# A new order of the first 170 steps of a fused attention and expert kernel

## The chip, the cores and the metric

One core of one Trainium2 chip runs the whole program. The metric is the time of one execution on the device in microseconds; the time before is the median of three runs.

## The reference

Eight sequences of 576 positions with 8 heads of 64 go through attention over a causal window of 64 positions. The result, 576 x 512 for each sequence, goes through one expert of eight: the mean over the positions picks the expert, and the whole sequence goes through it.

```
mask   = (rel >= 0) & (rel < 64)                     # rel = query position - key position
attn   = softmax(where(mask, q @ k.T / 8, -1e9))
x      = attn @ v                                    # heads side by side: (8, 576, 512)
e      = argmax(x.mean(axis=1) @ w_gate)             # one expert for each sequence
out[b] = prob[e] * (relu(x[b] @ w1[e]) @ w2[e])      # w1: 512 x 1024, w2: 1024 x 512
```

## The kernel before, in words

The program is a long list of short steps, `OPS`, written out as text. A loop at the end of the kernel takes the steps one by one, and each emits its instructions; every engine runs its own instructions in the order in which the list emits them. Waits are put in by the framework from the data, the buffers and the PSUM banks that the steps share. So the list is the schedule.

A batch `b` (a sequence) has five units: four pairs of heads for positions 0 to 511, and a tail unit for positions 512 to 575 of all heads. Units are counted through: unit 7 is pair 2 of batch 1, unit 9 the tail of batch 1. A step's name is a letter, sometimes the letter of an engine (`a` for ACT, `d` for DVE) or of a variant (`m`: the PSUM tile comes from the tag `mo` with three buffers and not from a tag with one; `b`: the mask is added by a matmul), and a number:

- Loads. `Qx` loads q (even x) or k (odd x) of batch x // 2, 512 KB in bf16, from GpSimd's queue; `Q0.48` loads heads 4 to 7 alone. `Y0.24` loads heads 2 and 3 of batch 0 in fp32 from SyncE's queue, and `Cd0.24` casts them. `Lx` loads a piece of v (five for a batch, the last of half the size), `tx` the tails of q and k (two transfers), `Wx` a quarter of the expert's weights (`W0` and `W1` of w1, `W2` and `W3` of w2 for batch 0). All but `Y` are issued by GpSimd.
- Set-up. `y`, `i`: the band of the mask and the identity, on GpSimd; `mb`, `Mb`, `z`: masks and zeroes on DVE.
- Attention of a unit. `T` transposes q and k on TensorE; `U` and `k` copy the transposed q and k out of PSUM; `S` makes the scores; `E` takes the exponentials (ACT); `K` multiplies by the mask (DVE), where `S` had no `b`; `l` sums the rows (TensorE); `n` and `R` make the reciprocal (ACT, a logarithm and an exponential); `A` multiplies by v (TensorE); `X` scales the result into `xm` (DVE). `Vb` copies v shifted by half a block, on DVE, and the main `A` steps of the batch need it.
- Gate of a batch. `g`, `j`, `G` pick the expert, `P` reads its number into a register of GpSimd, and the `W` steps of that batch can be issued only then.
- Experts. Each `c` is the next chunk of matmuls of the expert (line 461 and 470 for w1, 503 and 512 for w2), each `r` moves a finished chunk out of PSUM, each `O` stores a result.

What the prediction's steps touch are these rules of the buffers: the transposes without `m` share one PSUM buffer, the scores without `m` one pair of banks, the row sums one buffer (`lb`), the products without `m` one (`av`); `mo` has three, of which `S` with `m` takes two. Exponentials have four buffers, transposed q three.

```
        if 'm' in e:
            sp = [ps_m.tile([128, 512], FP32, tag="mo", name="s") for _ in range(2)]
...
        pe = apool.tile([128, 2, 8, 64], FP16, tag="pe", name="pe", bufs=4)
...
        nc.gpsimd.dma_start(
            out=tiles[b][:, lo:hi],
            in_=src[b, lo:hi, 0:SM].rearrange("h (p r) d -> p h (r d)", r=4))
```

Of the kernel before, what the change touches and what calls it, by code (L numbers as in the profile page):

```python
# [1 line left out]
OPS = (  # L2
    "Y0.24 Q0.48 Q1.48 Q0.2 Cd0.24 y i Q1.2 Y1.24 Q3 Cd1.24 z Tm3 Tm2 mb T0 Tm1 ka3 ka2 ka0 "
    "t0 Ud3 Ud2 Q2 Sb3 L0 L3 ka1 L1 L2 E3 Smb2 L4 Ud0 l3 Ud1 t1 S0 T4 E2 kd4 Ud4 n3 Smb1 E0 "
    "Mb K0 E1 R3 Q4 L9 Tm5 Sb4 Tm7 Tm8 Ud5 Q5 ka5 kd8 E4 L5 kd7 l1 n1 T6 l4 n4 Ud7 l2 Sb5 ka6 "
    "n2 R1 R4 l0 V0 A3 Ud6 L7 Am1 n0 E5 T9 X3 Am2 Ud9 S7 R2 L8 E7 Ud8 X1 R0 l5 X2 L6 n5 Smb6 "
    "A0 Am4 K7 ka9 E6 t2 X4 X0 Sb8 l7 g0 n7 T12 j0 Q6 Sm9 Tm10 G0 Ud12 kd12 E8 Ud10 H0 E9 "
    "Tm13 Tm11 R7 K9 l6 R5 ka10 Sb12 Ud11 ka13 V1 n6 Q7 l8 P0 Ud13 W0 I0 kd11 T14 Am5 A7 X7 "
    "A6 Ud14 kd14 L12 n8 X5 E12 R6 l12 n12 Sm14 X6 S11 l9 E14 Smb10 Tm17 E11 n9 T18 W1 Ud17 "
    "A9 W2 E10 S13 kd18 Ud18 L13 Tm15 Ud15 l10 Am8 R8 W3 kd15 ka17 T16 K14 L11 c X8 L14 n10 "  # L10
    "E13 R9 c ra X9 c R10 c rd c g1 K11 rd S17 j1 G1 ra ra c H1 L10 c rd l14 K13 c t3 ra c P1 "
    "n14 Q8 ra c c rd c V2 Ua16 c c ra ka16 l11 A10 X10 Am12 W4 c Q9 R12 X12 n11 ra W5 R11 "
    "A11 rd W6 T19 E17 c l13 n13 R13 Ua19 I1 X11 c Sm18 S15 K17 L15 rd E18 W7 R14 A13 c l17 "
    "ra X13 A14 c L16 L17 X14 g2 n17 Tm20 E15 ra kd19 c Ud20 ra L18 kd20 T22 S19 Sm16 E19 L19 "
    "j2 G2 c P2 t4 K15 E16 Q10 K18 c ra c W8 H2 ra ka22 c ra c c S20 l18 ra rd rd K16 c n18 "
    "Q11 K19 L21 ra Tm21 c c Ua21 Ud22 l16 W9 T23 R17 kd21 L23 V3 c c R18 c ra Am17 Ud23 n16 "
    "ra l15 E20 X17 L22 c R16 ka23 c rd n15 A18 c S23 X18 Sm21 K20 T24 kd24 ra R15 E21 L20 "
    "A16 c l19 L29 ra L24 W10 n19 Ud24 Am15 X16 A19 W11 R19 c X15 l20 E23 n20 L25 I2 c X19 rd "
    "L26 ra Tm26 c g3 K23 kd26 l23 Ud26 R20 c ra Sm22 n23 S24 j3 rd G3 E24 E22 T28 H3 K21 c "
    "Tm27 Ud28 P3 t5 ka27 kd28 l21 L28 rd n21 I3 K24 S26 L27 T25 c V4 W12 c Ua27 ra l24 c K22 "  # L20
    "c ra ra ra Ud25 n24 c R23 Q13 Q12 Am20 X20 R21 c c c rd Am23 W13 kd25 E26 A21 T29 rd X23 "
    "l22 Sm27 W14 W15 n22 E27 S28 V5 c c K26 K27 L32 c R24 l26 c X21 t6 A24 E28 Am22 ra R22 "
    "L30 ra K28 n26 X24 Ud29 kd29 c A27 l27 n27 c X22 ra ra c g4 S25 R26 rd Sm29 j4 G4 L34 "
    "E29 T32 Tm30 kd30 E25 Ud30 c Ua32 H4 K29 P4 ka32 ra c l28 R27 T33 L33 rd Ua33 S30 I4 n28 "
    "c Q15 c ra L31 ra Am26 ka33 c E30 c ra W16 X27 X26 ra l29 c K25 R28 c rd n29 Q14 A28 K30 "
    "c W17 X28 T34 S32 Sm33 ra O O E32 c E33 c K32 l25 n25 R25 c kd34 Am25 A29 W18 c O Ua34 "
    "R29 rd W19 T31 l30 c X29 X25 rd ka31 g5 c c Ud31 O ra K33 rd Sm31 n30 S34 j5 G5 c V6 R30 "
    "P5 rd O E31 H5 c K31 T36 l32 Ud36 rd E34 c t7 c A30 c n32 I5 rd L39 ka36 ra R32 l33 T35 "
    "X30 A32 Ua35 L38 rd c K34 rd c ka35 c n33 T37 ra Sm35 S36 L37 O E35 rd c X32 ra E36 W20 "
    "l34 c L35 n34 c K35 K36 L36 c kd37 R33 c O l31 rd W21 R34 rd c n31 R31 c Ua37 Tm38 O W23 "  # L30
    "Ud38 A33 ra ka38 Am34 l35 T39 X33 c n35 W22 c ra X34 A31 X31 g6 kd39 c O Sm38 R35 O S37 "
    "ra E38 j6 c c G6 P6 Ud39 E37 ra ra c V7 K38 rd H6 c l36 c K37 W24 n36 S39 A35 l37 ra rd "
    "E39 c ra n37 c X35 R36 c A37 c ra l38 Am36 K39 ra c c O R37 rd X37 n38 Am39 X36 O c rd c "
    "I6 l39 W27 R38 c n39 O O A38 rd R39 c W25 W26 ra X39 X38 g7 c j7 O c G7 c ra c P7 rd ra "
    "c c O W29 O c ra c O rd H7 O ra c O c W28 W31 ra O ra O c ra c c ra rd c c c c rd c W30 "
    "I7 O ra O c rd c c ra rd O c O O rd c O rd O O c rd c c O ra c c rd c O rd ra rd c c O "
    "rd O c c ra O O c c c c ra rd o O c ra O c ra o "
).split()

# [554 lines left out]
```

## Time and profile before

| | |
|---|---|
| median of the runs | 204.35 us (203.72, 204.35, 204.58) |
| profiled execution, its own time | 203.52 us |
| its span | 201.9 us |
| TensorE busy | 183.5 us, 91% of the span |
| ACT, DVE, GpSimd busy | 131.8, 119.9, 111.0 us |
| granted clock of TensorE | 0.996 |
| moved by DMA | 41.16 MB, 204 GB/s in the mean |

The profile is one execution. Its span runs from the first to the last instruction. A row of a timeline has the start from the beginning of the span, the length, the engine, the line of the kernel, the operation and its tiles, and in square brackets how long the engine sat idle ahead of it and what ended that. PE is TensorE's matmuls, PEld its loading of weights, POOL is GpSimd.

### The profile page before, as it was taken

What the parts mean: (1) busy time and instruction counts of PE and PEld (TensorE: products, weight loads), DVE (VectorE), ACT (ScalarE), POOL (GpSimd) and SP (SyncE); (2) the same over time, 40 slices, a digit from 0 to 9 for tenths busy, and PEclk for the clock granted to TensorE, in tenths of its full rate; (3) what the DMA queues carried; (4) which work ended last, traced back from release to release, by engine and by line L of the source; (5) the groups of instructions that cost most, each with busy time, mean ns of one, the idle gap of its engine ahead of it and who ended that gap; (6) DMA issues with size and microseconds to landing.
All of it is one profiled execution on the core that took longest, in us unless ns stands there. A gap on an engine that the chain in (4) does not pass through costs nothing.

```text
span 201.9 us, 8105 instructions
## 1 busy us (share of the span) xinstructions
PE 183.5 (91%) x3518; PEld 124.2 (62%) x3522; DVE 119.9 (59%) x347; ACT 131.8 (65%) x247; POOL 111.0 (55%) x158
## 2 busy tenths in 40 slices
PE   0487886899999999999999999999999999999991
PEld 0455564656677756577667666676656666776760
DVE  3527989595477546895877457966494651216410
ACT  2179998876599578977779975757787436321121
POOL 7985939235931593478633552439452716553561
PEclk9999999999999999999999999999999999999998
DMA  6999999999999999999999999999999999999693
GB/s 135 175 188 159 194 162 198 199 198 174 196 201 197 170 198 193 174 201 167 200 206 200 169 195 223 259 208 137 183 237 243 266 254 212 274 212 301 235 325 134
DMA packets 83346, 41.16 MB, mean 204 GB/s; under 512 B 48080, under 2 KB 80976, under 8 KB 83312
## 3 DMA queue, kind: packets, MB, share of 16 engines
q0 software_dynamic: 81936, 39.72, 138.5%
q1 hardware_dynamic: 768, 0.85, 1.3%
q8 instruction: 27, 0.44, 0.8%
q10 hardware_dynamic: 608, 0.08, 0.2%
q14 instruction: 7, 0.06, 0.1%
HBM read 61.88 MB, written 9.44 MB: 353 GB/s over the span
## 4 chain that ended last, share of the span: by engine, by line
PE 77%; DMA 9%; POOL 7%; issue 3%; DVE 2%; ACT 1%; POOLq 0%; DVEq 0%; ACTq 0%
PE ph L461 28%; PE po L503 25%; DMA vw<-in_v_dram 9%; PE tp L225 5%; PE ph L470 4%; PE s L275 4%; PE av L331 3%; PE po L512 3%; PE lb L309 3%; POOL vw L141 2%; POOL km L110 2%; POOL qm L110 1%; POOL out_dram L492 1%; PE gps L392 1%; POOL qkt L133 1%
## 5 line engine op out<-in xcount | busy, mean ns | idle before, releaser
L503 PE MATMUL po<-w2b,hm 128*64 128x512 f16 x512 | 60.1, 379 | 0.0
L461 PE MATMUL ph<-xm,w1b 128*64 128x512 f16 x512 | 60.0, 379 | 0.0
L461 PEld LDWEIGHTS <-w1b 128*64 128x64 f16 x512 | 31.7, 110 | 18.7 <-issue 0.4
L503 PEld LDWEIGHTS <-hm 128*64 128x64 f16 x512 | 30.1, 110 | 19.3
L141 POOL DMA_DIRECT2D vw<-in_v_dram x32 | 28.9, 910 | 13.3 <-DMA w1b<-in_moe_w_dram 4.3
L446 ACT ACTIVATE hm<-ph,gw 128x512 f16<-128x512 f32 x39 | 26.6, 693 | 13.4 <-PE ph L461 13.3
L492 POOL DMA_DIRECT2D out_dram<-ob x31 | 17.2, 557 | 25.0 <-DMA w1b<-in_moe_w_dram 7.0
L351 ACT ACTIVATE ln<-lb 128x512 f32<-128x512 f32 (+1 forms) x40 | 22.5, 563 | 11.8 <-PE lb L309 8.6
L364 DVE CUSTOM_DVE_ANT_0 xm<-av,rl 128x512 f16<-128x512 f32 x32 | 21.6, 686 | 10.4 <-PE av L331 9.5
L482 ACT COPY ob<-po 128x512 f32<-128x512 f32 x18 | 10.6, 586 | 23.6 <-PE po L503 23.6
L448 DVE TENSOR_SCALAR hm<-ph,gw 128x512 f16<-128x512 f32 x25 | 18.7, 748 | 12.1 <-PE ph L461 11.6
L357 ACT ACTIVATE rl<-ln 128x512 f32<-128x512 f32 (+1 forms) x40 | 23.3, 594 | 1.5 <-DVE pool L364 1.3
L225 PE MATMUL tp<-ident,qm 128*64 128x128 bf16 x256 | 13.8, 232 | 7.4 <-DMA qm<-in_q_dram 6.9
L288 ACT ACTIVATE pe<-s 128x1024 f16<-128x1024 f32 x19 | 19.5, 1028 | 1.4 <-PE s L275 0.7
L297 DVE TENSOR_TENSOR pe<-pe,mask 128x1024 f16<-128x1024 f16 x24 | 16.3, 687 | 3.9 <-ACT pe L288 3.1
L252 ACT COPY kT<-tp 128x512 bf16<-128x512 bf16 x19 | 11.2, 597 | 9.0 <-PE tp L225 8.0
L225 PEld LDWEIGHTS <-qm 128*64 128x64 bf16 x256 | 10.7, 118 | 10.0 <-DMA qm<-in_q_dram 6.9
L482 DVE COPY ob<-po 128x512 f32<-128x512 f32 x14 | 9.7, 690 | 10.7 <-PE po L503 10.5
L423 POOL DMA_DIRECT2D w1b<-in_moe_w_dram x16 | 12.6, 785 | 5.9 <-DMA vw<-in_v_dram 2.9
L275 PEld LDWEIGHTS <-kT 64*128 64x128 bf16 x576 | 10.1, 95 | 8.9 <-issue 5.6
L331 PEld LDWEIGHTS <-vw 128*64 128x64 f16 x512 | 12.4, 112 | 4.7 <-issue 1.2
L225 PE MATMUL tp<-ident,km 128*64 128x128 bf16 x256 | 13.9, 231 | 1.4 <-DMA km<-in_k_dram 0.9
(80 smaller groups left out, 267.2 us busy)
## 6 DMA issues: line engine op xcount, KB each, us to landing
w1b<-in_moe_w_dram POOLq DMA_DIRECT2D x16, 512.0 KB, 9.3
w2b<-in_moe_w_dram POOLq DMA_DIRECT2D x16, 512.0 KB, 13.4
out_dram<-ob POOLq DMA_DIRECT2D x31, 256.0 KB, 8.1
vw<-in_v_dram POOLq DMA_DIRECT2D x32, 128.0 KB, 9.0
km<-in_k_dram POOLq DMA_DIRECT2D x7, 512.0 KB, 9.3
qm<-in_q_dram POOLq DMA_DIRECT2D x7, 512.0 KB, 9.0
out_dram<-obt POOLq DMA_DIRECT2D x14, 64.0 KB, 7.7
qkt<-in_q_dram POOLq DMA_DIRECT2D x8, 64.0 KB, 7.6
```

The source lines that it names most:

```text
L141: nc.gpsimd.dma_start(out=vt[:, 2 * J + 1], in_=v[b, :, 128 * J:128 * J + 128].rearrange("h c d -> c h d"))
L225: nc.tensor.transpose(tp[p0:p0 + 64, n, r], t[:, 2 * i + hh, ts(r, 64)], ident)
L288: nc.scalar.activation(out=po, in_=sp[0], func=AF.Exp, scale=scale)
L351: nc.scalar.activation(out=ln, in_=lb[:, 0:n], func=AF.Ln)
L357: nc.scalar.activation(out=rl, in_=lns.pop((b, i)), func=AF.Exp, scale=-1.0)
L364: nc.vector.tensor_tensor_reduce(out=xm[:, i], in0=av.rearrange("q r p -> q (r p)"), in1=rl, scale=1.0, scalar=0.0, op0=ALU.mult, op1=ALU.add,
L446: nc.scalar.activation(out=o, in_=i, func=AF.Relu, scale=g)
L448: nc.vector.tensor_scalar(out=o, in0=i, scalar1=g, scalar2=0.0, op0=ALU.mult, op1=ALU.max)
L461: nc.tensor.matmul(out=ph[64 * c:64 * c + 64], lhsT=w1t[:, kb, ts(2 * ft + c, 64)], rhs=xm[:, kb], start=(kb == 0), stop=(kb == 3), skip_g ...
L482: copy(e)(out=ob, in_=po)
L492: (nc.scalar if n and eng is nc.sync else eng).dma_start(out=dst, in_=src)
L503: nc.tensor.matmul(out=po[64 * c:64 * c + 64], lhsT=hm[:, fb, ts(2 * r + c, 64)], rhs=w2t[:, fb], start=(fb == 0), stop=(fb == 7), skip_gr ...
```

## The change

The first 170 of the list's 890 steps are put in another order. They are the same steps; the other 720 keep their order behind them. Eighteen steps change a letter: the two casts `C` go from DVE to ACT; of the copies, `k3`, `k1`, `k5`, `k6` and `k9` go from ACT to DVE, and `U3`, `U8`, `k8` and `k11` from DVE to ACT; `T3`, `T8` and `S14` lose their `m`, `T6` gets one; of the products, `A3` and `A7` get an `m` and `A1` loses it.

GpSimd's order of the steps up to `W2`, before and after:

```
before  Q0.48 Q1.48 Q0.2 y i Q1.2 Q3 t0 Q2 L0 L3 L1 L2 L4 t1 Q4 L9 Q5 L5 L7 L8 L6 t2 Q6 Q7 P0 W0 L12 W1 W2
after   Q0.48 i Q1.48 t0 Q1.2 y Q0.2 L2 Q2 Q3 L4 L0 L3 L1 t1 Q4 L9 Q5 L6 L8 L7 L5 t2 Q6 Q7 P0 W0 W1 L12 W2
```

The diff, up to the place from which both lists are the same (`S13 kd18 Ud18 L13` and on, which is only broken into other lines):

```
-    "Y0.24 Q0.48 Q1.48 Q0.2 Cd0.24 y i Q1.2 Y1.24 Q3 Cd1.24 z Tm3 Tm2 mb T0 Tm1 ka3 ka2 ka0 "
-    "t0 Ud3 Ud2 Q2 Sb3 L0 L3 ka1 L1 L2 E3 Smb2 L4 Ud0 l3 Ud1 t1 S0 T4 E2 kd4 Ud4 n3 Smb1 E0 "
-    "Mb K0 E1 R3 Q4 L9 Tm5 Sb4 Tm7 Tm8 Ud5 Q5 ka5 kd8 E4 L5 kd7 l1 n1 T6 l4 n4 Ud7 l2 Sb5 ka6 "
-    "n2 R1 R4 l0 V0 A3 Ud6 L7 Am1 n0 E5 T9 X3 Am2 Ud9 S7 R2 L8 E7 Ud8 X1 R0 l5 X2 L6 n5 Smb6 "
-    "A0 Am4 K7 ka9 E6 t2 X4 X0 Sb8 l7 g0 n7 T12 j0 Q6 Sm9 Tm10 G0 Ud12 kd12 E8 Ud10 H0 E9 "
-    "Tm13 Tm11 R7 K9 l6 R5 ka10 Sb12 Ud11 ka13 V1 n6 Q7 l8 P0 Ud13 W0 I0 kd11 T14 Am5 A7 X7 "
-    "A6 Ud14 kd14 L12 n8 X5 E12 R6 l12 n12 Sm14 X6 S11 l9 E14 Smb10 Tm17 E11 n9 T18 W1 Ud17 "
-    "A9 W2 E10 S13 kd18 Ud18 L13 Tm15 Ud15 l10 Am8 R8 W3 kd15 ka17 T16 K14 L11 c X8 L14 n10 "
...
+    "Y1.24 Q0.48 i Q1.48 t0 Y0.24 Ca1.24 T3 Ca0.24 Q1.2 Tm2 z y Q0.2 mb L2 Tm1 kd3 Ud2 kd1 Q2 "
+    "Ua3 T0 Sb3 ka2 Q3 Smb2 Ud0 ka0 E3 S0 E2 l3 n3 Ud1 Smb1 E1 L4 L0 T4 L3 E0 R3 kd4 Tm5 L1 "
+    "Mb Ud4 Ud5 Tm6 Tm7 l1 Ud6 Sb4 n1 K0 kd6 E4 kd7 T8 ka8 l2 n2 kd5 l4 Sb5 t1 Ua8 n4 Q4 R1 "
+    "L9 l0 V0 T9 Am3 Q5 R4 A1 Ud7 n0 L6 X3 E5 X1 L8 R2 Am2 R0 S7 l5 Ud9 X2 A0 kd9 E7 Smb6 n5 "
+    "Am4 E6 Sb8 L7 X0 K7 l7 X4 L5 T12 g0 n7 Sm9 j0 t2 Tm10 G0 Q6 E8 ka10 Ud12 E9 kd12 Q7 P0 "
+    "H0 R5 Tm11 Sb12 l6 Tm13 Ud10 Ud11 V1 R7 T14 ka11 n6 Am5 Ud14 kd14 l8 ka13 I0 Am7 W0 Ud13 "
+    "E12 S14 n8 W1 X7 E14 A6 X5 R6 l12 Smb10 S11 K9 X6 n12 l9 L12 E11 Tm17 T18 A9 W2 n9 E10 "
+    "Ud17 S13 kd18 Ud18 L13 Tm15 Ud15 l10 Am8 R8 W3 kd15 ka17 T16 K14 L11 c X8 L14 n10 E13 R9 "
+    "c ra X9 c R10 c rd c g1 K11 rd S17 j1 G1 ra ra c H1 L10 c rd l14 K13 c t3 ra c P1 n14 Q8 "
...
```

53 rows, old and new, of the table OPS are left out of this document.

## The prediction

> **What bounds the kernel now.** I read the page first, then the windows on both sides of the first expert matmul, then the chain of work that ended last, and only then the loads one by one. The page gives the length:
>
> ```profile
> span 201.9 us, 8105 instructions
> ```
>
> The windows view (start:end, its length, then busy time of PE, PEld, DVE, ACT, POOL, the granted clock, DMA share, GB/s) shows which engine fills it, and where not:
>
> ```profile
> 0.00:42.00 42.00, 28.00 (x694) 20.21 (x700) 26.77 (x82) 30.43 (x56) 30.20 (x43) 1.00 1.57 177
> 42.00:196.00 154.00, 153.91 (x2808) 102.91 (x2806) 93.15 (x266) 100.38 (x190) 79.75 (x113) 1.00 1.40 212
> ```
>
> From 42 us on TensorE is busy 153.91 of 154 us: no order of the rest can bring anything there. All that a new order of the first 170 steps can touch is the head, 14 us of idling in the first 42 us, and its whole effect on the time is how much sooner or later TensorE begins the unbroken stretch. The marker is the first expert matmul, `c` number one on line 461. The chain of work that ended last (start, length, what) shows what the head hangs on:
>
> ```profile
> 9.54 9.13 DMA vw<-in_v_dram
> ...
> 22.68 8.52 DMA vw<-in_v_dram
> 31.32 0.88 DVE vw L150
> ...
> 41.01 4.32 PE ph L461 x40
> ```
>
> It is a chain of loads: a v load that lands at 18.67, another issued at 22.68 that lands at 31.20, then DVE's shift `V1`, then some 8 us of attention work to 41.01 (the chain counts from when a step was free of its predecessor; the first `c` itself starts at 40.84, below).
>
> **The loads are one line of transfers.** GpSimd issues of the timeline, and the landing times (last column, from issue) of the same transfers:
>
> ```profile
> 8.67 0.91 POOL L141 DMA_DIRECT2D vw<-in_v_dram  x1
> ...
> 12.59 0.69 POOL L145 DMA_DIRECT2D vw<-in_v_dram  x1 [0.39 <-DMA km<-in_k_dram]
> ...
> 27.82 0.88 POOL L110 DMA_DIRECT2D km<-in_k_dram  x1 [1.72 <-DVE grd L384]
> 30.04 0.75 POOL L423 DMA_DIRECT2D w1b<-in_moe_w_dram  x1 [1.34 <-DVE kT L252]
> ```
>
> ```profile
> vw<-in_v_dram POOLq DMA_DIRECT2D x1, 128.0 KB, 8.1
> vw<-in_v_dram POOLq DMA_DIRECT2D x1, 64.0 KB, 8.1
> km<-in_k_dram POOLq DMA_DIRECT2D x1, 512.0 KB, 9.0
> w1b<-in_moe_w_dram POOLq DMA_DIRECT2D x1, 512.0 KB, 9.4
> ```
>
> `Q7` is issued at 27.82 and lands at 36.8, `W0` at 30.04 and lands at 39.4: issued 2.2 us apart, landed 2.6 us apart. 512 KB drain in 2.6 us, and the other 6 to 7 us are spent behind what was issued before. So a load lands when the bytes ahead of it in GpSimd's issue order are through, whatever the moment of its issue, as long as the line doesn't run dry.
>
> **The change part by part: the queue.** The list of GpSimd transfers ahead of `W0` has 26 entries, and it is the same 26 afterwards. Counted through: after the ninth the bytes are equal (before: four pieces of batch 0's q and k, `Q3`, `t0` twice, `Q2`, `L0`; after: the same with `L2` for `L0`, of the same size), after the thirteenth the sets are equal, and from the fourteenth on the order is the same up to three places inside batch 1's v (`L5` to `L8`, all four needed by `V1`). Hence:
> - `Q3` (k of batch 1) moves from fifth to ninth and lands where `L0` did, 8.67 + 8.1 = 16.8.
> - The last piece of batch 0's v is now the thirteenth, `L1`, and lands where `L4` did, 12.59 + 8.1 = 20.7.
> - batch 1's v stays complete at 31.2, `Q7` lands at 36.8, `W0` at 39.4. Nothing of this moves.
> - `i` (0.24 us in the chain) now stands ahead of `Q1.48`, and `y` behind `Q1.2`. With a full line behind it, that costs nothing; dry, at most its own 0.24 us, which every later landing would inherit. I take 0.
> - `W1` passes `L12`, both behind `W0`: one lands earlier, the other later by the length of the first, and `c` needs neither.
>
> **What changes engine, and the start.** ACT's and DVE's first copies out of the transposes, and the group of k copies on DVE (its mean in ns behind the comma):
>
> ```profile
> 9.09 0.58 ACT L252 COPY kT<-tp 128x512 bf16<-128x512 bf16 x1 [6.35 <-PE tp L225]
> ```
>
> ```profile
> 9.70 0.42 DVE L242 COPY qt<-tp 128x512 bf16<-128x512 bf16 x1 [2.33 <-ACT kT L252]
> ```
>
> ```profile
> L252 DVE COPY kT<-tp 128x512 bf16<-128x512 bf16 x13 | 8.8, 684 | 2.8 <-PE tp L225 1.9 <-ACT qt L242 0.9
> ```
>
> The two casts go from DVE to ACT. No row shows a cast on ACT; its copy of that width takes 0.58 us, and it is idle for 6.35 us before the first one, so two casts are hidden, and so is the changed order of the two SyncE loads that they read (0 us; without the idle time 1.2 us). Of the copies, `k3`, `k1`, `k5`, `k6` and the small `k9` go to DVE, `U3`, `U8`, `k8` and `k11` to ACT: ACT loses one copy net (under 0.6 us), DVE gains four times 0.68 and the small one and gives up 2 x 0.68 + 2 x 0.42 = 2.2, so under 1 us more. Neither sum is on the path, which hangs on the loads of v; without that cover DVE's 1 us would count. The second row shows something else: `Ud3` reads the same PSUM tile as `ka3` and begins 0.03 us after it ends, so the two copies of a tile take turns. Afterwards unit 3 sits in the one-buffer tag `tp` and its copies are `kd3` on DVE and `Ua3` on ACT, again in turn, and `T0` must wait for both: 9.09 + 0.68 + 0.58 makes 10.35. But `T0` now stands behind `Tm1`, which keeps TensorE until about 10.4. Cost 0; if the turn takes longer, a few tenths, ahead of slack that comes next.
>
> **Batch 1's transposes and batch 0's shift.** `Tm5` needs `Q3`. TensorE's row before:
>
> ```profile
> 15.94 0.41 PE L225 MATMUL tp<-ident,qm 128*64 128x128 bf16 x8
> ```
>
> With a landing at 16.8 it moves back by 0.9 us, and ACT's score work on batch 1 with it. `V0` starts after the last piece of v:
>
> ```profile
> 20.34 0.89 DVE L150 COPY vw<-vw 64x2048 f16<-64x2048 f16 x1 [0.54 <-DMA vw<-in_v_dram]
> ```
>
> It goes from 20.34 to about 20.8, and with it the gate of batch 0, `P0` and the issue of `W0`, 30.04 to 30.5 at the latest. `W0` spends 9.4 us from issue to landing, 2.6 of them draining, so half a microsecond of later issue is covered several times. Without the cover it would cost 0.5 us.
>
> **The end of the head.** Here the terms fall. ACT's and TensorE's rows from the shift `V1` to the first `c`:
>
> ```profile
> 32.91 0.60 ACT L351 ACTIVATE ln<-lb 128x512 f32<-128x512 f32 x1 [0.56 <-PE lb L309]
> 33.46 1.02 ACT L288 ACTIVATE pe<-s 128x1024 f16<-128x1024 f32 x1
> 34.79 0.63 ACT L357 ACTIVATE rl<-ln 128x512 f32<-128x512 f32 x1 [0.31 <-DVE pool L364]
> 35.51 0.60 ACT L351 ACTIVATE ln<-lb 128x512 f32<-128x512 f32 x1
> 36.00 0.66 ACT L291 ACTIVATE pp<-s 128x256 f16<-128x256 f32 x2
> 36.53 1.04 ACT L288 ACTIVATE pe<-s 128x1024 f16<-128x1024 f32 x1
> 37.43 0.42 ACT L351 ACTIVATE ln<-lb 128x256 f32<-128x256 f32 x1
> 37.69 1.14 ACT L291 ACTIVATE pe<-s 128x512 f16<-128x512 f32 x2
> ```
>
> ```profile
> 37.26 0.41 PE L225 MATMUL tp<-ident,qm 128*64 128x128 bf16 x8
> ...
> 38.68 0.38 PE L225 MATMUL tp<-ident,km 128*64 128x128 bf16 x7 [0.50 <-issue]
> ...
> 39.45 0.41 PE L225 MATMUL tp<-ident,qm 128*64 128x128 bf16 x8
> ...
> 40.84 0.60 PE L461 MATMUL ph<-xm,w1b 128*64 128x512 f16 x4
> ```
>
> `E12` at 33.46 reuses the exponentials' buffer that `Am5` reads, and `Am5` waits for `V1`; so v's landing at 31.2 sets it in both orders. From there ACT runs `E12`, `n8`, `E14`, `R6`, `n12`, `E11`, `n9`, `E10` afterwards. The eight durations add up to 6.11 us, and successive rows overlap by some 0.13 us each (36.53 + 1.04 against 37.43), so 5.2 us: `E10` can end at 38.7; `R6` now waits for the later of two products on DVE, so I keep 38.8, which is also the value before (37.69 + 1.14 = 38.83). `Tm15` writes a PSUM buffer that `E10` frees, so it can start at 38.9 in both orders. Before it starts at 39.45. The half microsecond between is the row at 38.68: TensorE sat 0.50 us in the middle of `T18` waiting for nothing that the profile shows. From `Tm15` to `c` it is 40.84 - 39.45 = 1.39 us of dense work, four steps (`Tm15`, `l10`, `Am8`, `T16`) that keep their order.
>
> So what the new order gains is decided by `T17`, which started at 37.26 though `Q7` had landed at 36.8, and by the 0.50 us. TensorE reaches `T17` afterwards at 36.9, when `Q7` lands. If the stall belongs to a point in TensorE's instruction list (the same number of instructions lies ahead of it in both orders) and ends at 38.68 again, `c` stays at 40.84 and the gain is 0. If it moves with TensorE, by up to 0.4 us, `c` comes at 40.45. If it vanishes, `Tm15` starts at 38.9 and `c` at 40.3, a gain of 0.5 us. I take the middle of the first two, 0.2 us, because the profile has one such stall and nothing to say that it depends on the order.
>
> A page row bears on it, a queue that carries instructions, 16 KB a packet:
>
> ```profile
> q8 instruction: 27, 0.44, 0.8%
> ```
>
> [...]
>
> **The sum.** `c` from 40.84 to 40.64, everything behind it unchanged: 203.5 - 0.2 = 203.3 for a run like the profiled one (its time stands 1.6 us over its span). The median of the runs is 204.35, 0.8 above the profiled execution, and the runs range from 203.72 to 204.58; so 204.15 for the median. A measurement can tell about 0.5% (1.0 us) from no change here, and the sum is a fifth of that.
>
> **The rivals.**
> - *The stall vanishes* (0.22): `c` at 40.3, 203.85. For it: one stall in 201.9 us. Against it: both orders have the same instruction count there. Still within 0.5%.
> - *Faster: the first weights become the bound* (0.12). If ACT gets through earlier, because `E10`'s end or the buffer of `E12` was not what held `Tm15`, `c` can follow `W0` at 39.4: 1.4 us less, 202.95. Against it: `E12` hangs on v's landing at 31.2, which the order can't move.
> - *Slower: batch 1's k comes too late* (0.18). The chain above has one v load landing at 18.67, while the one issued ahead of it landed at 16.8: 1.9 us apart, while the next 320 KB, to `L4` at 20.7, took 2.0 us, 0.8 for 128 KB. Such a jump of 1 us may hit `Q3` in its new place: 17.8 instead of 16.8, and `Tm5` comes 1.9 us later than before. ACT's only spare time behind it is the 0.56 us ahead of `n8`. What goes beyond that shifts `E12` to `E10` and `c`: 1.9 - 0.6 = 1.3 us, 205.65. Against it: ACT would have to be late all the way from `E5` on. It makes the kernel slower by over 0.5% from a start of `Tm5` at 15.9 + 0.6 + 1.0 = 17.5 on.
> - *The order doesn't bring the head forward at all* (the stall ends at 38.68 again): 204.35; it is one end of the forecast and has no chance of its own.
>
> **How the numbers follow.** Forecast 0.48, stall gone 0.22, faster 0.12, slower 0.18. The first two are within 0.5%: 0.70. Their own range is 203.3 to 204.6 (0 to 0.5 us of gain, and runs from 0.6 under to 0.2 over their median). The range for all reaches down to 203.1, near the faster rival, and up to 205.6, the slower one, and leaves out less than 2 in 10.
>
> **What would show it.** Right: the loads of `Q7` and `W0` land within 0.3 us of 36.8 and 39.4; `V0` starts near 20.8; `Tm5` near 16.8; `E10` ends near 38.8; the first row of line 461 starts between 40.3 and 40.9; TensorE stays gapless behind it. Wrong: `W0` lands over 0.5 us earlier or later, so that the landings follow more than the bytes ahead; an ACT wait of over 0.6 us between `E5` and `E12`; a TensorE wait behind 42 us, which would say that loads now come too late for it.

## The result, and the profile after

The changed kernel takes 204.58 us in the median of 22 runs (203.87 to 206.63), the kernel before 203.88 us beside it on the same chip (22 runs). The ratio is 1.0037, 95% interval 1.0020 to 1.0054: slower by about 0.7 us. The forecast was 204.15 us, a gain of 0.2. The time lies in the range and within the 0.5% called "same", but it moved the other way, by more than the interval leaves to chance.

The profiled execution took 204.44 us, 0.92 more than that of before. Its length, and the windows on both sides of 42 us:

```profile
span 202.8 us, 8110 instructions
```

```profile
0.00:42.00 42.00, 27.86 (x690) 19.56 (x692) 26.45 (x80) 30.68 (x55) 29.64 (x42) 1.00 1.56 176
42.00:196.00 154.00, 153.91 (x2807) 102.34 (x2805) 94.00 (x268) 101.33 (x191) 80.42 (x114) 1.00 1.40 210
```

TensorE is as gapless behind 42 us as before (153.91 of 154 us in both). So in these two profiles the 0.9 us lie in the head. TensorE's rows there, from batch 1's first transposes to the first `c`:

```profile
16.43 0.39 PE L225 MATMUL tp<-ident,qm 128*64 128x128 bf16 x8
17.93 0.41 PE L225 MATMUL tp<-ident,km 128*64 128x128 bf16 x8 [1.11 <-DMA km<-in_k_dram]
...
37.60 0.41 PE L225 MATMUL tp<-ident,qm 128*64 128x128 bf16 x8
...
38.27 0.22 PE L225 MATMUL tp<-ident,km 128*64 128x128 bf16 x1
39.52 0.41 PE L225 MATMUL tp<-ident,km 128*64 128x128 bf16 x7 [1.03 <-issue]
...
40.32 0.41 PE L225 MATMUL tp<-ident,qm 128*64 128x128 bf16 x8
...
41.71 1.03 PE L461 MATMUL ph<-xm,w1b 128*64 128x512 f16 x8
```

The first `c` starts at 41.71 instead of 40.84: +0.87, the whole difference of the two spans. Two rows are new in kind. Inside `Tm5` TensorE waits 1.11 us for batch 1's k, and the break in `T18` has grown from 0.50 to 1.03 us. The chain of waits (start, length, what) tells where the delay begins:

```profile
8.54 9.35 DMA km<-in_k_dram
...
17.93 0.43 PE tp L225 x8
...
19.26 0.60 DVE pe L297
19.86 1.05 DVE kT L252 x2
...
21.00 0.66 DVE kT L252
...
21.68 1.19 DVE vw L150
...
22.91 0.95 DVE vw L151
...
24.32 1.03 ACT pe L288
```

and `E5` in the kernel before:

```profile
22.68 1.02 ACT L288 ACTIVATE pe<-s 128x1024 f16<-128x1024 f32 x1
```

Before, the chain ran over two loads of v. Now it runs over `Q3`, which is issued at 8.54 and lands at 17.89; then over copies on DVE, three of k among them (`kd6`, `kd7`, `kd5`); then over DVE's shift `V0`, which begins at 21.68 though the last piece of batch 0's v is complete at 20.86; and so to `E5` on ACT, at 24.32 instead of 22.68. From there to 40 us no gap of ACT is longer than 0.15 us. What is left of the delay at its end:

```profile
34.29 1.02 ACT L288 ACTIVATE pe<-s 128x1024 f16<-128x1024 f32 x1
...
37.41 1.02 ACT L288 ACTIVATE pe<-s 128x1024 f16<-128x1024 f32 x1
...
38.60 1.09 ACT L291 ACTIVATE pe<-s 128x512 f16<-128x512 f32 x2
```

`E5` is 1.64 us late, `E12` 0.83 (34.29 against 33.46), `E10` ends 0.86 late (39.69 against 38.83), and `c` comes 0.87 late. The last link is the break in `T18`: in the chain it stands from 38.49 to 39.52, and dense work follows it up to `c`.

The later loads went nearly as forecast. GpSimd's issues of `Q7` and of `W0` with `W1`, and the time from issue to landing of the first two:

```profile
28.03 0.88 POOL L110 DMA_DIRECT2D km<-in_k_dram  x1 [1.77 <-PE al L339]
31.49 1.83 POOL L423 DMA_DIRECT2D w1b<-in_moe_w_dram  x2 [2.58 <-DVE kT L252]
```

```profile
km<-in_k_dram POOLq DMA_DIRECT2D x1, 512.0 KB, 9.0
w1b<-in_moe_w_dram POOLq DMA_DIRECT2D x1, 512.0 KB, 8.1
```

`Q7` lands at 37.1 (36.8 before) and `W0` at 39.6 (39.4), though `W0` is issued 1.45 us later: the line hid that.

**Why `Q3` lands at 17.9.** The trace has 16 completions for each transfer (an expectation below speaks of 16 rings for them). First and last completion of the loads in question, worked out from these records (us from the start):

```
                       Q2 first   last     Q3 first   last    last - first, Q3
before                   15.0     15.8       11.5     12.3        0.8
before, second profile   15.0     16.5       11.5     13.0        1.5
after                    13.3     15.2       16.1     17.9        1.8
after, second profile    13.3     16.2       16.0     18.9        2.9
after, third profile     13.3     15.4       16.0     18.5        2.5
L0 of before (Q3's place now): first 15.9, last 16.8
```

The first completion of `Q3` comes at 16.0 to 16.1 in all three profiles, only 0.2 us behind that of `L0` before. The rest is the last completion, 1.8 to 2.9 us behind the first where `L0` had 0.9. In the order after, small transfers (`t0`, `Q1.2`, `Q0.2`, `L2`) stand at the head. They drain in 0.43 to 0.84 us each while GpSimd needs 0.7 to 0.9 us to issue one, so the line is nearly or quite empty when `Q2` is issued at 7.67: its first completion comes 3.2 us behind that of the transfer ahead, where 512 KB take 2.66 us in a full line (`Q2` before, 12.36 to 15.02). The lag of the last completion is not the work of that gap alone: in the first profile it was 1.65 us from the second transfer on.

### The profile page after: what moved, and what is told of

Same layout as the page of the kernel before. It is cut to its first block, busy times and chain, and to the rows that moved or that the text cites. A ratio compares the mean times of both kernels' runs of the same rounds, so it can differ in the third digit from the quotient of the medians.

```text
span 202.8 us, 8110 instructions
## 1 busy us (share of the span) xinstructions
PE 184.3 (91%) x3522; PEld 123.7 (61%) x3522; DVE 121.1 (60%) x346; ACT 133.0 (66%) x247; POOL 111.2 (55%) x158
## 4 chain that ended last, share of the span: by engine, by line
PE 65%; DMA 14%; POOL 6%; issue 5%; ACT 4%; DVE 3%; POOLq 1%; DVEq 0%
PE ph L461 21%; PE po L503 20%; PE tp L225 5%; DMA w2b<-in_moe_w_dram 5%; DMA w1b<-in_moe_w_dram 5%; DMA km<-in_k_dram 5%; PE s L275 4%; PE av L331 4%; PE ph L470 3%; PE lb L309 3%; POOL out_dram L492 3%; PE po L512 2%; ACT pe L288 2%; POOL qm L110 1%; ACT ln L351 1%
## 5 line engine op out<-in xcount | busy, mean ns | idle before, releaser
L275 PEld LDWEIGHTS <-kT 64*128 64x128 bf16 x576 | 10.4, 96 | 9.9 <-issue 7.5
L291 ACT ACTIVATE pe<-s 128x512 f16<-128x512 f32 x26 | 14.1, 597 | 1.2 <-PE s L275 1.2
L426 POOL DMA_DIRECT2D w2b<-in_moe_w_dram x16 | 12.4, 781 | 4.3 <-DMA km<-in_k_dram 2.0
```

## The experiments

Theory 1: the order of the loads does it; batch 1's k comes late and everything behind it with it. Theory 2: TensorE's break in `T18` does it; it belongs to a place in the instruction list, has grown to 1.03 us, and sets `c`. Each kernel was measured beside the kernel before on the same chip.

**Only the old loads' order.** The order after for every step but the loads (and `y` and `i` between them), which are issued as before:

```diff
-Q0.48 i Q1.48 t0 Q1.2 y Q0.2 L2 Q2 Q3 L4 L0 L3 L1 t1 ...
+Q0.48 Q1.48 Q0.2 y i Q1.2 Q3 t0 Q2 L0 L3 L1 L2 L4 t1 ...
```

> The changed kernel, with the order of the loads (and of the two mask steps) on SyncE and GpSimd put back to the one before, W0 included; every other engine keeps the changed order. Theory 1, the loads: the keys of batch 1 (Q3) land at 15.8 or sooner instead of 17.9, Tm5 starts near 16.0, ACT's chain E12 to E10 comes back by 0.8 us, and the first expert matmul starts near 40.8 instead of 41.7, so the time is that of the kernel before, ratio 0.998 to 1.002. Rival, the compute order: the new order on TensorE, ACT and DVE is itself slower, the first expert matmul stays at 41.5 or later, ratio 1.003 to 1.005.

204.11 us against 204.12, ratio 0.9989 [0.9954, 1.0024]: the loss is gone. The profiled execution, at 204.54 us one of the longer ones:

```profile
16.80 0.41 PE L225 MATMUL tp<-ident,qm 128*64 128x128 bf16 x8 [0.72 <-DMA qm<-in_q_dram]
...
38.31 0.41 PE L225 MATMUL tp<-ident,km 128*64 128x128 bf16 x7 [0.28 <-issue]
```

`Tm5` runs in one piece, `E12` starts at 33.69, and `c` at 40.50, earlier than before. In this execution that doesn't shorten the time; among other things TensorE later waits for weights:

```profile
152.42 1.05 PE L461 MATMUL ph<-xm,w1b 128*64 128x512 f16 x8 [0.52 <-DMA w1b<-in_moe_w_dram]
```

**Only the new loads' order.** The kernel before with the loads issued in the order after (the diff above the other way round).

> The kernel before, with the changed order of the loads on SyncE and GpSimd alone. Theory 1, the loads: Q3 lands at 17.5 to 18, Tm5 starts 2 us later than before, and the first expert matmul moves from 40.8 to 41.5 or later, ratio 1.003 to 1.006. Rival, the compute order: the first expert matmul stays within 0.2 us of 40.8, ratio 0.999 to 1.001.

204.86 us, ratio 1.0049 [1.0017, 1.0080]: the whole loss. `E12` starts at 34.20, `E10` ends at 40.18, `c` starts at 41.93. But in this profile it is not `Q3` that does it. `Q3` lands at 17.04 (its last completion only 0.9 behind the first), and `Tm5` runs from 16.85 on without a wait for it. Three other things are seen. The chain of waits starts from `Q0.2`, the last piece of batch 0's q, issued at 6.15 instead of 3.09 and landing at 9.81 instead of 8.97. TensorE works at the slower pace of its start for longer (in the kernel before a group of eight transposes takes 0.64 us from 6.88 to 10.97 and 0.41 at 15.94): the same group of scores takes 0.61 us as late as 14.18, and 0.41 in the kernel before at 13.39.

```profile
14.18 0.61 PE L275 MATMUL s<-qt,kT 64*128 64x64 bf16 x16
15.29 0.41 PE L275 MATMUL s<-qt,kT 64*128 64x64 bf16 x16
```

```profile
13.39 0.41 PE L275 MATMUL s<-qt,kT 64*128 64x64 bf16 x16
```

And the granted clock (the third number from the end) stands at 0.50 between 36 and 39 us, where it is 1.00 in the kernel before:

```profile
36.00:39.00 3.00, 3.00 (x48) 1.45 (x46) 1.05 (x4) 2.50 (x6) 1.25 (x2) 0.50 1.24 206
```

`E12` is 0.74 late ahead of that; what `E10` and `c` lose beyond it falls into the slow stretch. There is no break in `T18`, but that says little against theory 2: slowed down, TensorE comes to the place some 2.9 us after an instruction fetch has begun (36.86), later than the 2.24 to 2.45 us at which the breaks told of below end. So the two runs show that the loads' order carries the loss. They don't show that it does so through `Q3`.

**43 short matmuls at the start**, ahead of everything on TensorE, into a spare bank of PSUM, to shift the instruction list; once in the kernel before, once in the one after. A step `F43.64` stands for 43 matmuls of 64 columns.

```diff
-    "Y0.24 Q0.48 ...
+    "F43.64 Y0.24 Q0.48 ...
```

> The kernel before, with 43 more matmuls of 64 columns on a tile of zeroes at the very start of TensorE's list, where it waits for the first load until 6.9 us; their result is used by nobody. They move every later block border of 256 instructions forward by 86. Theory 2, the stall in T18 is a fetch of instructions: it is gone from T18, Tm15 starts at 38.9 and the first expert matmul at 40.3 instead of 40.8, ratio 0.997 to 0.998. Rival: the stall hangs on something else; it stays in T18, 0.4 to 1.0 us long, ratio 0.999 to 1.001.

> The changed kernel with the same 43 small matmuls ahead. Theory 2: the 1.0 us of stall in T18 is gone, E10 (end 39.7) then holds Tm15, and the first expert matmul starts near 41.15 instead of 41.7, ratio to the kernel before 1.000 to 1.002. Rival: the stall stays, ratio 1.003 to 1.005.

Ratios 1.0109 [1.0069, 1.0149] and 1.0165 [1.0122, 1.0209]. The break left `T18`, as theory 2 said, and came back 128 matmuls later in the list (kernel before with 43):

```profile
40.32 0.60 PE L461 MATMUL ph<-xm,w1b 128*64 128x512 f16 x4
42.04 2.32 PE L461 MATMUL ph<-xm,w1b 128*64 128x512 f16 x19 [1.12 <-issue]
```

`c` starts 0.5 us earlier, and its first chunk breaks after four matmuls. So the break does belong to a place: behind matmul 601 + 128 k of the trace (605 where four more are recorded), every 128 matmuls with their 128 weight loads. That is 256 instructions; the trace of before has 27 fetches of 16 KB for 3518 matmuls and 3522 weight loads, one for 261 in the mean. Moving it brought nothing.

**20 short matmuls**, in the kernel before and in the order after with the old loads' order.

```diff
-    "Y0.24 Q0.48 ...
+    "F20.64 Y0.24 Q0.48 ...
```

> The kernel before with 20 small matmuls of zeroes at the start of TensorE's list in place of 43. The run with 43 moved the stall by whole blocks of 128 matmuls, into the first chunk of the expert. With 20 the two block borders fall at the start of T17 (instructions ahead of it spread over 2.2 us) and 23 matmuls into the first chunks. Theory 2, a fetch takes 2.3 to 2.45 us from its start, some 40 matmuls ahead of the border: at most 0.2 us of stall at T17 and none at the second, Tm15 starts at 38.9 and the first expert matmul at 40.3, ratio 0.997 to 0.999. Rival, more instructions or a later border cost time whatever their number: ratio over 1.003, as with 43.

> The changed order on TensorE, ACT and DVE, the order of the loads as before (the kernel that came out even with the kernel before), and 20 small matmuls ahead. If theories 1 and 2 both hold and add up: first expert matmul at 40.0 to 40.2, ratio 0.995 to 0.998. Rival, W0's landing at 39.4 to 39.8 or the E10 chain holds it: not under 40.4, ratio 0.998 to 1.001.

1.0120 [1.0081, 1.0160] and 1.0082 [1.0051, 1.0113]. In the kernel before the break is now longer, not gone:

```profile
39.03 0.27 PE L225 MATMUL tp<-ident,qm 128*64 128x128 bf16 x3 [0.99 <-issue]
```

The instruction queue that the prediction showed fetches 16 KB each time (0.44 MB in 27 packets), and the last fetch ahead of this border began at 36.61, 2.42 us ahead of the end of the break. In the other profiles with a break there the distance is 2.24 to 2.45 us (before: 36.23 to 38.68; after: 37.26 to 39.52). That TensorE waits there for the fetch is the author's reading of these distances; no row shows the wait's releaser. In the changed kernel the fetch began 1.03 us later and the break ended 0.84 later, about as much as `c`. What sets the start of the fetch was not traced, and so it stays open how much of the 0.87 us would go with the break.

**3 long matmuls**, the control: 3 instructions and 1.46 us of TensorE time, more than the 20 short ones take (1.25) and less than the 43 (2.47).

```diff
-    "Y0.24 Q0.48 ...
+    "F3.512 Y0.24 Q0.48 ...
```

> A control for the fills: the order before with 3 matmuls of 512 columns at the start, ahead of everything else, which write a spare PSUM bank that nothing reads; about as long in TensorE time as the 43 matmuls of 64 columns in the earlier run, but only 3 instructions further in the list. If the fill's position in the list did the harm (blocks of 128 matmuls): the stall stays in T18 with 0.4 to 0.6 us, c within 0.3 us of 40.84, ratio 1.000 to 1.003. If the work itself at the start did the harm (it delays the loads or the first transposes): ratio about 1.011, as with 43 short ones.

0.9987 [0.9961, 1.0013]; the break stays in `T18`, `c` at 40.91. So with 20 it is the shift of the list that cost 1%, not the work; for 43 the control is too short to say it by itself.

**`Q3` alone moved**: in the order after it changes places with `L2`; in the kernel before it goes behind `L0`.

```diff
-Q0.48 i Q1.48 t0 Q1.2 y Q0.2 L2 Q2 Q3 L4 ...
+Q0.48 i Q1.48 t0 Q1.2 y Q0.2 Q3 Q2 L2 L4 ...
```

```diff
-Q0.48 Q1.48 Q0.2 y i Q1.2 Q3 t0 Q2 L0 L3 ...
+Q0.48 Q1.48 Q0.2 y i Q1.2 t0 Q2 L0 Q3 L3 ...
```

> The changed kernel with two loads changed about: Q3 (keys of batch 1, 512 KB) in the place of L2 and L2 (128 KB of batch 0's v) in the place of Q3; nothing else. Theory 1, Q3's place: q and k of batch 1 are both in by about 16, Tm5 ends near 16.7, ACT's chain comes back by 0.8 us or more and the first expert matmul starts between 40.4 and 41.0; ratio 0.996 to 1.001. Rival, the rest of the queue's new order (t0 ahead, the mask steps between the loads): the first expert matmul stays at 41.5 or later, ratio 1.003 to 1.005.

> The kernel before with one load moved: Q3 from the fifth to the ninth place, behind L0, as in the changed kernel; all else as before. Theory 1: Q3 lands near 16.9, Tm5 starts 1 to 2 us later, and the first expert matmul comes 0.5 to 1.2 us later, ratio 1.003 to 1.006. Rival: the 0.56 us of idle time on ACT ahead of n8 covers it, ratio 0.999 to 1.001.

The first: `Q3` at 14.12, `E12` at 33.11, `E10` ends at 38.52, `c` at 40.51, 1.2 us earlier than after. The time doesn't follow: 204.52 us, ratio 1.0040 [1.0003, 1.0076]. Two rows of its profile:

```profile
40.51 1.68 PE L461 MATMUL ph<-xm,w1b 128*64 128x512 f16 x14
...
96.91 0.84 PE L503 MATMUL po<-w2b,hm 128*64 128x512 f16 x6 [0.49 <-issue]
```

From `c` to the last matmul it is 157.65 us here against 156.5 before and 156.6 after: so 1.05 of the 1.2 us was given back behind `c`, 0.49 of it in the break shown; the rest was not traced. The loss stays although `Q3` and `c` are early.

In the second the late `Q3` costs most, 206.99 us, ratio 1.0135 [1.0087, 1.0183]:

```profile
16.24 0.41 PE L225 MATMUL tp<-ident,qm 128*64 128x128 bf16 x8
19.40 0.41 PE L225 MATMUL tp<-ident,km 128*64 128x128 bf16 x8 [2.75 <-DMA km<-in_k_dram]
...
45.00 1.25 PE L461 MATMUL ph<-xm,w1b 128*64 128x512 f16 x10
```

The line ran dry at `Q2` and `Q3`, the last completion fell from 0.95 to 2.6 us behind the first, k landed at 19.36, and `c` started 4.2 us late. The granted clock fell too: 0.66 in the mean from 20 to 25 us. So 4.2 us is the price of the late k and of the low clock together.

**`t0` behind `Q2`**, in the order after:

```diff
-Q0.48 i Q1.48 t0 Q1.2 y Q0.2 L2 Q2 Q3 L4 ...
+Q0.48 i Q1.48 Q1.2 y Q0.2 L2 Q2 t0 Q3 L4 ...
```

> The order after, with two loads moved in GpSimd's queue: Q2 comes straight behind L2, and t0 (the tails of q and k, 2 x 64 KB) behind Q2 instead of ahead of Q1.2. Q2 is then issued about 1.4 us earlier (near 6.3 instead of 7.67), with less in the line ahead of it. Theory 1 (a line that runs dry behind small early transfers makes batch 1's k late): the 0.56 us dry ahead of Q2 goes, Q3 lands near 17.2 instead of 17.9, Tm5 starts near 17.2 without a break of a microsecond in its middle, and c starts between 41.0 and 41.4 instead of 41.7; time 0.3 to 0.7 us under that of the order after, ratio to before about 1.001. Theory 2 (the late end of TensorE's stall, an instruction fetch, sets c): c is as late as in the order after within 0.2 us, ratio about 1.004. Rival: one of the 16 rings lags as before whatever the order, so that Q3 is still complete only at 17.7 or later; c then also stays late.

204.11 us, ratio 1.0028 [0.9998, 1.0058]. The first completion of `Q2` comes at 12.2 and that of `Q3` at 15.8, the latter 0.3 earlier than after; but the last was 2.3 us behind, so `Q3` was complete at 18.07, as the rival said. In this profile the clock fell, to 0.80 in the mean from 15 to 20 us and 0.86 from 20 to 25:

```profile
18.11 0.64 PE L225 MATMUL tp<-ident,km 128*64 128x128 bf16 x8 [1.93 <-DMA km<-in_k_dram]
```

A transpose group of 0.41 us takes 0.64, and `c` starts at 42.62. The time is between before and after, and the interval holds both "no loss" and "all of it".

**Both kernels again**, for what changes from execution to execution.

> The order before once more, for a second profile: how far c and the landings scatter from execution to execution. Expected: c within 0.3 us of 40.84, Q3 12.3 to 12.9, Tm5 15.9 to 16.8, a stall of about 0.5 us in T18; span 201.6 to 202.9.

> The order after once more, for a second profile. Theory 1 expects the line dry ahead of Q2 again (0.4 to 0.7 us), Q3 complete after 17.2, Tm5's end after 17.7, c between 41.3 and 41.9. If Q3's late landing was an accident of the one profiled execution: Q3 at 16.8 to 17.0 and c at or before 41.0.

> The order after a third time, as the measure for the run beside it: ratio 1.002 to 1.0055 again, about two thirds of its executions under a mean clock of 0.998. Its profile shows which kind it is: with a wait for batch 1's k of under 1.2 us the clock stays at 1.00 and c starts between 41.3 and 41.9; with a wait of over 1.8 us it falls to 0.5 to 0.8 behind it and c starts after 42.5.

Before: 203.48 us, `Q3` 12.97, `Tm5` 16.57, a break of 0.23 us in `T18`, `c` 40.99. After: 207.46 us with `Q3` complete at 18.91 and `c` at 44.70; and in the third measurement 204.85 us, ratio 1.0055 [1.0030, 1.0081], with these rows of TensorE and these windows in its profile (in the windows the granted clock is the third number from the end):

```profile
15.41 0.41 PE L225 MATMUL tp<-ident,qm 128*64 128x128 bf16 x8 [0.38 <-DMA qm<-in_q_dram]
18.53 0.64 PE L225 MATMUL tp<-ident,km 128*64 128x128 bf16 x8 [2.71 <-DMA km<-in_k_dram]
```

```profile
15.00:20.00 5.00, 1.92 (x38) 1.73 (x38) 1.34 (x5) 2.24 (x4) 2.12 (x3) 0.77 2.09 163
20.00:25.00 5.00, 4.04 (x74) 2.33 (x70) 4.65 (x8) 3.67 (x8) 4.97 (x7) 0.89 1.62 190
```

The 0.77 and 0.89 are means over 5 us; from 18 to 21 us the view gives 0.50. So the profile of the result shows the mild kind, and there is a worse one. Of 35 timed or profiled executions of the changed kernel, 12 had a mean clock of 0.994 or less, median 205.4 us, and 9 one of 0.998 or more, median 204.1. Of 102 of the kernel before it was 11 (205.2 us) and 58 (203.6 us), leaving out one of 245 us. At full clock the change costs about 0.5 us; low clocks come three times as often with it (34% against 11%). Both figures put several measurements and chips together, and the kernel before alone went from none of 22 with a low clock in one measurement to 6 of 22 in another.

**TensorE kept at work during the wait**: 6 matmuls of 512 columns directly ahead of `Tm5` in the order after.

```diff
-... kd4 Tm5 L1 Mb ...
+... kd4 F6.512 Tm5 L1 Mb ...
```

> The order after with 6 matmuls of 512 columns put on TensorE directly ahead of Tm5 (they write a spare PSUM bank that nothing reads): some 1.3 us of work at the place where TensorE waits for batch 1's k. They cost nothing as long as k is complete later than about 17.9, since the transposes of q move into the time that was spent waiting for k. Theory A (part of the loss is the clock: TensorE sits idle until k is there and the granted clock falls for some 10 us in part of the executions): the wait inside Tm5 shrinks to 0 to 1.0 us, the granted clock of the first 42 us is 1.00, fewer executions than before lie under a mean clock of 0.998 (15 of 22 did), and the median falls by 0.3 to 0.6 us against the order after, ratio to before about 1.001. Theory B (only k's landing counts; the clock's fall is unrelated to this wait): ratio 1.003 to 1.005 and the same share of executions with a lower clock. Rival: the 6 more instructions shift the border of TensorE's instruction blocks and cost more than they save: ratio over 1.006.

```profile
15.91 1.47 PE L550 MATMUL wps<-warm 128*128 128x512 bf16 x6
17.31 0.41 PE L225 MATMUL tp<-ident,qm 128*64 128x128 bf16 x8
17.77 0.41 PE L225 MATMUL tp<-ident,km 128*64 128x128 bf16 x8
```

```profile
20.00:25.00 5.00, 3.39 (x112) 2.40 (x106) 4.67 (x11) 4.93 (x10) 4.56 (x6) 1.00 1.60 192
```

None of 12 executions had a mean clock of 0.994 or less; of the changed kernel beside it 6 of 12. So in this order the wait for k brings the clock down, and work in the wait keeps it up (1.00 from 20 to 25 us here, 0.89 in the profile above). It isn't the only thing that does: with `Q3` early 4 of 12 executions had such a clock, and so had 4 of 12 with only the new loads' order, whose profile has no wait for k. And the median only went from 204.85 to 204.58, ratio 1.0050 [1.0027, 1.0072]: theory B's number with theory A's clock. `c` started at 40.97 in the profile, about as early as before, and from there to the last matmul it took 157.4 us. Like `Q3` early, this run has an early `c` and keeps the loss. What its 6 more matmuls cost by shifting the list was not measured apart.

**One copy of k back to ACT**, in the order after:

```diff
-... l2 n2 kd5 l4 Sb5 ...
+... l2 n2 ka5 l4 Sb5 ...
```

> The order after with one letter changed: kd5, the last of three copies of batch 1's k that stand ahead of V0 on DVE (19.77 to 21.65 in the profile of the changed kernel, V0 starting behind them at 21.68 though v was complete at 20.86), goes to ACT as ka5. Theory A (the late k does its harm by these copies, which now push back V0 and with it E5): V0 starts at 21.0 to 21.2 where k lands as in the first profile, E5 0.3 to 0.6 us earlier than its 24.32, E10's end up to 0.5 us earlier than 39.69; median 0.2 to 0.5 us under the order after's, ratio 1.001 to 1.004. Theory B (ACT is the bound from E4 on, and 0.6 us more on ACT takes back what DVE gives): V0 earlier, E5 not; c and the time as in the order after, ratio 1.004 to 1.006.

204.23 us against 203.53, ratio 1.0057 [1.0024, 1.0090] (the two medians alone would give 1.0034, as those of the result do): no better that could be told. Its profile is one with a fallen clock (0.58 from 20 to 25 us, `Q3` at 18.93), so its rows can't be set beside those of the first profile. That DVE's copies carry the delay in that one is shown by the chain alone; that taking one away helps is not shown.

## Why the prediction was wrong

Two steps of the working failed: the landing of `Q3`, and the step by which a later `Tm5` costs nothing because `E12` hangs on `V1`'s load. In the order of the prediction:

- *TensorE is unbroken from 42 us, so the start of `c` decides.* Right for the two profiles compared first: `c` +0.87, span +0.9. As a general rule it was too simple. The order after with an early `c` (40.50, 40.51, 40.97) took 157.4 to 157.9 us from there to the last matmul, the kernel before 156.3 to 156.5 (two profiles, `c` at 40.84 and 40.99). Two of these three runs kept the loss (ratios 1.0040 and 1.0050), so it is not shown that a late `c` is what the medians lose. "Everything behind it unchanged" in the sum was not a safe step.
- *The landings follow the bytes ahead.* Right where the line was full: the last v piece 20.86 (forecast 20.7), batch 1's v 30.90 (31.2), `Q7` 37.08 (36.8), `W0` 39.59 (39.4), and 1.45 us of later issue of `W0` were covered.
- *`Q3` lands where `L0` did, 16.8.* **This step failed**: 17.89, in other profiles of the same kernel 18.5 and 18.9. The condition "as long as the line doesn't run dry" stood in the text and was not worked out. The dry line ahead of `Q2` (bound 0.24, measured 0.56) is the smaller part; the larger is the last of the 16 completions, 1.8 to 2.9 us behind the first where the row of `L0` had 0.9 in it. The landing of one transfer in one profile was taken for a property of its place.
- *Engines that change.* The casts cost nothing on the path, as forecast; `T0` started at 10.94, not 10.4, and nothing hung on it. "DVE under 1 us more, not on the path" was wrong once k was late: three copies of k stood ahead of `V0` on DVE, and `V0` started at 21.68, not 20.8.
- *`E12` is set by V1's load, `E10` ends at 38.8.* **This step failed with it**, and it is why a later `Tm5` was priced at nothing. The sum of the ACT steps was right (5.2 us forecast, 34.29 to 39.69 measured: 5.4). Its start was not: `V1` came at 32.33 instead of 31.32 though its load was 0.3 us earlier, and `E12` at 34.29. In the kernel before, the load landed at 31.19, and the copy ahead of `V1` on DVE, which waits for TensorE, ended at 31.18. The two chains ended together, so there was next to no slack behind the load for anything late ahead of it. DVE's rows before, and after:

```profile
30.76 0.42 DVE L242 COPY qt<-tp 128x512 bf16<-128x512 bf16 x1 [0.30 <-PE tp L225]
31.32 0.87 DVE L150 COPY vw<-vw 64x2048 f16<-64x2048 f16 x1
```

```profile
31.88 0.42 DVE L242 COPY qt<-tp 128x512 bf16<-128x512 bf16 x1 [0.29 <-PE tp L225]
32.33 0.69 DVE L150 COPY vw<-vw 64x2048 f16<-64x2048 f16 x1
```

With only the new loads' order `Tm5` started at 16.85, as forecast, its v landed at 30.6, and `E12` was still 0.74 late.

- *The 0.5 us break is worth 0 to 0.4.* It neither vanished nor moved forward; it grew to 1.03 us and ended 0.84 later. The view that it belongs to a place in the list was right: in most profiles of the study it showed behind matmul 601 (0.18 to 1.05 us).
- *The slower rival*, "batch 1's k comes too late", is what happened in the profile of the result, down to its landing (17.8 forecast, 17.89 measured). That the figure fits so well is luck: with this order of the loads `Q3` landed anywhere from 17.04 to 18.93. Its price of 1.3 us was above the 0.87 of the profile, because `Tm5`'s first half didn't wait and ACT made up 0.8 us between `E5` and `E12`. It was given 0.18 against the claim that ACT would have to be late all the way from `E5` on: ACT was.
- *What stays open.* The order of the loads carries the loss; that is shown by exchanging it in both kernels. That it does so through `Q3` and `c` is shown for one profile by its chain, and two runs with an early `c` that kept the loss speak against it as the whole of the 0.7 us.

## What to carry to other kernels

A load moved behind others should be costed by the last of its 16 completions, over several executions (with this order of the loads that of `Q3` came from 17.04 to 18.93), and each issue should be checked for whether the line is still full when it comes: here it ran dry behind small early transfers, which drained in 0.43 to 0.84 us each and took 0.7 to 0.9 us to issue. A load moved later needs slack for that scatter, and where TensorE waits for it, for a lower clock behind the wait (here 0.50 behind waits of 1.93 to 2.75 us). Where a step is priced at nothing because it is hidden behind another chain, the slack of that chain should be read from its rows; here it was about 0.1 us. Time won ahead of a dense stretch is only won if that stretch keeps its length; it should be checked from the marker to the end, not only up to the marker.

## What the runs showed of the hardware that was not expected

- TensorE's breaks without a releaser in `T17`, `T18` and the first chunk stand at places 128 matmuls apart in the list (behind 601 and 729), and those whose fetch was read end 2.24 to 2.46 us after a 16 KB instruction fetch has begun. They reach 1.12 us inside a dense run of matmuls in the kernel before with 43 matmuls ahead, and 2.00 in the order after with 43 matmuls ahead. Why the stretch behind `c` loses 1 us in one order and not in another stayed open.
- The last of a transfer's 16 completions comes 0.53 to 2.34 us behind the first for the loads issued in the first 32 us of the two profiles compared first. For `Q3`, two of the 16 were over 1 us behind in the first profile of the changed kernel, five in the second, none in the kernel before. In the second profile of the changed kernel the lag jumped from 0.7 us at `Q0.2` to 2.9 at `Q2`, where the line was nearly dry, and then mostly stayed (2.9 us still at `Q7`). What sets it was not found.
- The granted clock fell to 0.50 behind waits of 1.93 to 2.75 us inside `Tm5` (six profiles), for 3.4 us in four of them (with `Q3` late, 0.66 in the mean from 20 to 25 us) and for 6.8 and 10.2 us in the others. It stayed at 1.00 behind one of 1.11 us there. The length of a wait alone doesn't decide it: with only the new loads' order the clock stood at 0.50 from 35.8 to 39.2 us behind a wait of 1.08 us, and behind the same wait it stayed at 1.00 in the kernel before. What decides it was not found.
